# Partition layout of the split keys, a third unit summed by TensorE in batch 1, and a start number for each head

## The chip, the cores and the metric

The kernel runs on one core of one Trainium2 chip. The metric is the device time of one execution in microseconds (us). Before the change three runs gave a median of 877.85 us (877.54 to 879.45).

Five engines work at once, each through its own stream of instructions, and wait for one another by semaphores. PE is TensorE (matrix products, output to the PSUM banks), DVE is VectorE, ACT is ScalarE, POOL is GpSimd, SP is SyncE, which here only starts DMA transfers. ACT starts some too.

## The reference

Four batches, eight heads each, 1152 tokens, head size 64. Neighbouring queries are averaged, so that a head has 576 queries and 1152 keys. What follows the attention is a low-rank mix over tokens and a two-layer MLP.

```python
q_pool = q.reshape(B, H, S // factor, factor, D).mean(axis=3)
scores = scale * np.matmul(q_pool, k.transpose(0, 1, 3, 2))
scores = scores - np.max(scores, axis=-1, keepdims=True)
attn = np.exp(scores)
attn = attn / (np.sum(attn, axis=-1, keepdims=True) + 1e-09)
o = np.matmul(attn, v)                 # heads side by side: x is [4, 576, 512]
h = xt @ U @ V                         # xt is x transposed; U is [576, 32]
u = x + h.transpose(0, 2, 1)
out = u + np.maximum(u @ w_ch1, 0.0) @ w_ch2    # w_ch1 is [512, 2048]
```

## The kernel before

**Split numbers.** PE multiplies in a rounded format. To keep precision an operand is split in a high part (a rounded copy) and a low part (the operand minus the copy), and products of parts are summed in PSUM. For the scores, `T1` holds the high part of the keys in 64 of its 128 partitions and the low part in the other 64; `Q1` holds the high part of the queries twice, in both halves, so that one product (L758) gives high times high plus high times low whichever half holds which. The second product (L759) takes `T2`, the high keys once more and a row of ones, against `Q2`, the low queries and a row with minus the maximum.

**A head** (`head`, n = 8 times batch plus head) goes through these steps. From n = 8 on ("squares"), q and k are loaded as squares of 32 and turned by DVE (L535, L639); ACT copies the turned keys to `T3` (L640), which has one buffer; for each half z ACT writes the high part into `T1` (L643) and DVE or POOL the low part (L644); ACT starts a DMA from `T1` to `T2` (L649). ACT writes `Q1` (L577 to L578, shown as L393), DVE the low queries into `Q2` (L588). PE scans all scores in blocks for their maxima (L695, L697), DVE reduces each block (L701, L706), and a small DMA carries the row of maxima to `Q2`. Then come the scores (L758, L759), ACT's exponential into nine units of 128 keys (L765), the sum of units on DVE or POOL (`add`, L738) and the product with v (L790). Units that `add` leaves out (`LOOSE` of them) are summed by PE, with `ones` as weights, in `total` (L781), once for two heads. L818 and L827 turn the result, L830 to L854 divide it into `X`.

**The tail** of a batch (`tail`) does the low-rank mix (L881 to L903) and then the MLP (L973 on). The MLP of batches 0 to 2 is laid between the heads of the next batch; that of batch 3 stands alone at the end. The weights are decoded from 64-bit input in pieces (`decode`, L429 to L437) during batch 0's MLP.

**The order.** Every step is given to a planner (`Plan`) with a due number `at`, its possible engines with a cost each, and what it reads and writes. The planner replays the program with these costs, takes at each moment the ready step with the lowest due number (`slack` and `bias` bend this), and fixes for each engine the order of its instructions. `dual` offers a step to DVE and POOL. `begin(n)` is the due number at which head n starts and `T` counts from it. So a change of any number can move any instruction. For n < 16 the adds are dealt out by hand: units 1 to 3 go to POOL, the others to DVE.

Of the kernel before, what the change touches and what calls it, by code (L numbers as in the profile page):

```python
# [234 lines left out]
def kernel(  # L235
# [32 lines left out]
    FG = 2  # L268
    QT, KS = -9.2903, -10.0600
    LEAD = 53946.6, 7930.8  # L270
    WHOLE_KEYS, SPLIT = (False, False, True, True), 8
# [3 lines left out]
    TSW, TOT, TSL = 340.0, 325.0, -190.0  # L275
    SUM, AV, YT = 0.6238, 1.1450, 0.7203
# [6 lines left out]
    KT, MX0, MXS = 0.8419, -9.1810, 4.5042  # L283
    V_LO = slice(2 * R, 3 * R)
# [3 lines left out]
    SCALE = 0.5 / float(D) ** 0.5  # L288
    HEAD0, HEAD = 18071.4, 20721.3
    SLOT = HEAD / NG  # L290
    MLP_START, MLP_RATE = 4.9800, (2.0860, 2.0192, 1.7787, 2.0443)
    DEC_START, DEC_LEAD = 84755.4, 14620.3
    SLACK = 16.6000
# [85 lines left out]
    def v_(n):  # L379
        return 1.04 * n + 67  # L380
# [128 lines left out]
    def head(n):  # L509
        op = plan.op if n < len(heads) - 4 else lambda at, ways, r=(), w=(), port=False: plan.op(at, ways, [*r, *arena], w, port)  # L510
        b, h = heads[n]
        par = b % 2
        T = lambda G: begin(n) + G * (SLOT if n >= NWHOLE else SLOT * HEAD0 / HEAD)
        whole = WHOLE_KEYS[b] and not (n >= SQUARES)
# [8 lines left out]
        if squares:  # L523
            qr = lambda: qt.t[:, 0:2 * HALF].rearrange("p (m r d) -> p m r d", r=2, d=32)
            qs = lambda: qt.t[:, 0:HALF]
            for r in range(2):
                for e in range(2):
                    for c in range(2):
                        a = 32 * (2 * e + c)
                        op(T(-17), ("sp", SMALL * dma(36864), lambda a=a, e=e, c=c, r=r: nc.sync.dma_start(  # L530
                            qr()[a:a + 32, :, r], q[b, h, e * NQ:(e + 1) * NQ, 32 * c:32 * c + 32].rearrange("(m p r) d -> r p m d", p=32, r=2)[r]), 0, 1500, BULK), go if n > 1 else [], [(qt, a, r)])
            q_in = [(qt, 32 * a, r) for a in range(4) for r in range(2)]
            op(T(KS - 1), dual(HALF, lambda e: e.tensor_tensor(
                qp.t[:, 0:HALF].rearrange("p (m d) -> p m d", d=32), qr()[:, :, 0], qr()[:, :, 1], op=ALU.add)), q_in, [qp])
            op(T(KS), ("dve", v_(HALF), lambda: nc.vector.transpose(qs(), qp.t[:, 0:HALF])), [qp], q_in)  # L535
# [44 lines left out]
        for e in range(2):  # L580
# [50 lines left out]
        if squares:  # L631
            kr = lambda: kt.t.rearrange("p j (x d) -> p (j x) d", d=32)
            kq = lambda: ks.t.rearrange("p j d -> p (j d)")
            for z in range(2):
                for c in range(2):
                    a = 32 * (2 * z + c)
                    op(T(-17), ("sp", SMALL * dma(73728), lambda a=a, z=z, c=c: nc.sync.dma_start(
                        kr()[a:a + 32], k[b, h, z * S // 2:(z + 1) * S // 2, 32 * c:32 * c + 32].rearrange("(m p) d -> p m d", p=32)), 0, 1800, BULK), go, [(kt, a)])
            op(T(KS + 0.5), ("dve", v_(S // 2), lambda: nc.vector.transpose(kq(), kt.t.rearrange("p j d -> p (j d)"))), [(kt, 32 * a) for a in range(4)], [ks])  # L639
# [184 lines left out]
        def t3():  # L824
# [34 lines left out]
    def tail(b, clock):  # L859
# [339 lines left out]
```

## Time and profile before

| what | value |
|---|---|
| median of 3 runs | 877.85 us |
| the profiled execution, its own time | 877.02 us |
| its span, first to last instruction | 875.2 us |
| PE busy | 864.2 us, 99% |
| DVE busy | 742.4 us, 85% |
| ACT busy | 492.8 us, 56% |
| POOL busy | 252.9 us, 29% |
| granted TensorE clock | 1.000 |

Busy time of PE is not PE at its peak: matrix products are pipelined and their ends are modelled, so that a short wait between two of them can hide in it. The stages are best told apart by stretches of time: heads of batch 0 alone up to about 170 us, then heads of the next batch with the MLP of the one before up to about 700 us, then the MLP of batch 3. A chain of waits follows the work that ended last back from the end, and names for each moment the engine that everything later hung on.

### The profile page before, as it was taken

What the parts mean: (1) busy time and instruction counts of PE and PEld (TensorE: products, weight loads), DVE (VectorE), ACT (ScalarE), POOL (GpSimd) and SP (SyncE); (2) the same over time, 40 slices, a digit from 0 to 9 for tenths busy, and PEclk for the clock granted to TensorE, in tenths of its full rate; (3) what the DMA queues carried; (4) which work ended last, traced back from release to release, by engine and by line L of the source; (5) the groups of instructions that cost most, each with busy time, mean ns of one, the idle gap of its engine ahead of it and who ended that gap; (6) DMA issues with size and microseconds to landing.
All of it is one profiled execution on the core that took longest, in us unless ns stands there. A gap on an engine that the chain in (4) does not pass through costs nothing.

```text
span 875.2 us, 15732 instructions
## 1 busy us (share of the span) xinstructions
PE 864.2 (99%) x5405; PEld 701.7 (80%) x5405; DVE 742.4 (85%) x1508; ACT 492.8 (56%) x1127; POOL 252.9 (29%) x245
## 2 busy tenths in 40 slices
PE   9999998999999999999999999999999999999998
PEld 8787776787777777878888887888887778899987
DVE  8899999999999999978888878788886456798885
ACT  6788978847876876744545555554554322322220
POOL 3445554434443446521211112321402000001110
PEclk9999999999999999999999999999999999999999
DMA  5244645556866776754454453354643325555432
GB/s 172 80 132 110 179 125 136 122 158 185 230 198 190 205 207 186 204 133 121 109 151 104 102 147 95 86 139 122 176 119 102 119 97 185 180 191 191 168 107 99
DMA packets 186646, 128.23 MB, mean 147 GB/s; under 512 B 148139, under 2 KB 161734, under 8 KB 186566
## 3 DMA queue, kind: packets, MB, share of 16 engines
q1 hardware_dynamic: 183942, 117.95, 46.9%
q10 hardware_dynamic: 2624, 9.28, 4.6%
q8 instruction: 43, 0.70, 0.3%
q14 instruction: 37, 0.30, 0.1%
HBM read 96.17 MB, written 21.50 MB: 134 GB/s over the span
## 4 chain that ended last, share of the span: by engine, by line
PE 90%; DVE 5%; ACT 2%; DMA 2%; issue 1%; POOL 0%; SPq 0%; DVEq 0%; ACTq 0%
PE m L1122 22%; PE m L1007 17%; PE m L790 14%; PE s L758 8%; PE s L759 8%; PE m L695 8%; PE s L1051 6%; PE m L781 2%; DVE mp L701 1%; PE m L818 1%; PE m L697 1%; PE m L886 1%; DVE acc L738 1%; PE m L973 1%; PE m L668 1%
## 5 line engine op out<-in xcount | busy, mean ns | idle before, releaser
L765 ACT ACTIVATE big<-s 128x320 f32<-128x320 f32 (+2 forms) x448 | 196.5, 478 | 121.3 <-PE s L759 118.1
L701 DVE TENSOR_REDUCE mp<-m 128x1 f32<-128x384 f32 (+1 forms) x448 | 215.6, 534 | 36.8 <-PE m L695 35.4
L1122 PE MATMUL m<-w,hh 128*128 128x512 f32 x798 | 219.2, 394 | 0.0
L1007 PE MATMUL m<-rest,w 128*128 128x512 f32 (+1 forms) x768 | 178.6, 354 | 0.0
L758 PE MATMUL s<-room 128*128 128x256 f32 (+2 forms) x576 | 166.7, 305 | 0.5
L759 PE MATMUL s<-room 65*128 65x256 f32 (+2 forms) x576 | 163.9, 298 | 1.3 <-DMA room<-mr 1.3
L1122 PEld LDWEIGHTS m<-w,hh 128*128 128x128 f32 x798 | 145.3, 188 | 24.6 <-issue 0.9
L790 PE MATMUL m<-big,v 128*64 128x288 f32 x1152 | 148.5, 410 | 0.1
L1007 PEld LDWEIGHTS m<-rest,w 128*128 128x128 f32 x768 | 131.0, 188 | 13.8 <-issue 1.1
L790 PEld LDWEIGHTS m<-big,v 128*64 128x64 f32 x1152 | 79.1, 137 | 58.5 <-issue 6.8
L695 PE MATMUL m<-room 128*128 128x384 f32 x384 | 122.6, 356 | 2.8 <-DVE acc L738 1.3
L738 DVE TENSOR_TENSOR acc<-acc,big 128x576 f32<-128x576 f32 x133 | 102.7, 772 | 22.9 <-ACT big L765 17.1
L738 POOL TENSOR_TENSOR acc<-acc,big 128x576 f32<-128x576 f32 x67 | 95.6, 1426 | 85.1 <-ACT big L765 57.6
L758 PEld LDWEIGHTS s<-room 128*128 128x128 f32 x576 | 109.2, 190 | 10.8 <-issue 3.5
L759 PEld LDWEIGHTS s<-room 65*128 65x128 f32 x576 | 109.2, 190 | 6.7 <-DMA room<-mr 1.2
L695 PEld LDWEIGHTS m<-room 128*128 128x128 f32 x384 | 69.4, 188 | 23.8 <-issue 5.1
L1126 DVE TENSOR_TENSOR X<-m,X 128x512 f32<-128x512 f32 x95 | 65.0, 684 | 9.9 <-PE m L1122 9.6
L437 POOL TENSOR_TENSOR wt<-wt,rx 128x512 int32<-128x512 int32 (+2 forms) x35 | 45.5, 1302 | 68.8 <-DVE room L588 12.7
L583 POOL CAST qb<-room 64x64 fp32r<-64x64 f32 x54 | 17.7, 328 | 146.7 <-DVE acc L738 71.0
L799 ACT ACTIVATE ay<-m 128x256 f32<-128x256 f32 x48 | 18.4, 383 | 58.2 <-PE m L790 54.1
L1011 ACT ACTIVATE hh<-m 128x512 fp32r<-128x512 f32 (+1 forms) x64 | 32.9, 515 | 27.4 <-PE m L1007 26.4
L738 POOL TENSOR_TENSOR acc<-big 128x576 f32<-128x576 f32 x21 | 30.0, 1427 | 51.1 <-ACT big L765 50.9
(136 smaller groups left out, 1093.2 us busy)
## 6 DMA issues: line engine op xcount, KB each, us to landing
w<-wc SPq DMA_DIRECT2D x96, 512.0 KB, 4.0
rx<-in_moe_w_ch_dram SPq DMA_DIRECT2D x32, 512.0 KB, 4.1
wc<-w SPq DMA_DIRECT2D x32, 512.0 KB, 3.3
v<-in_v_dram SPq DMA_DIRECT2D x32, 288.0 KB, 3.0
room<-room ACTq DMA_DIRECT2D x31, 288.0 KB, 3.2
k<-in_k_dram SPq DMA_DIRECT2D x96, 72.0 KB, 2.2
q<-in_q_dram SPq DMA_DIRECT2D x192, 36.0 KB, 2.4
out_dram<-X SPq DMA_DIRECT2D x11, 256.0 KB, 2.6
```

What stands on the lines that cost most here:

```text
L437: op(at, ("pool", g_(n), lambda: nc.gpsimd.tensor_tensor(tv(), tv(), lo(), op=ALU.add)), [t, (raw, 1)] + use, [t])
L695: nc.tensor.matmul(pm.t[:, 0:w], Q1.t[:, t * P - 64:t * P + 64], T1.t[:, cs_], start=True, stop=True)
L701: op(T(MX0 + 0.3 + MXS * u / 14), ("dve", v_(w), lambda c=c, t=t, w=w, pm=pm: nc.vector.reduce_max(mp.t[:, c * 5 + t:c * 5 + t + 1], pm.t[ ...
L738: ways = dual(NQ, lambda e: e.tensor_tensor(acc.t, a(), b_(), op=ALU.add))
L758: nc.tensor.matmul(o, T1.t[:, kc], Q1.t[:, qa:qz], start=True, stop=False)
L759: nc.tensor.matmul(o, T2.t[:, kc], Q2.t[:, PAD + qa:PAD + qz], start=False, stop=True)
L765: op(T(when + 0.1), ("act", a_(len(js) * nq, True), lambda js=js, qa=qa, qz=qz, nq=nq, ss=ss, p=pu[j], e=js[0] % 2: nc.scalar.activation(p ...
L790: nc.tensor.matmul(pa.t[hf * D:(hf + 1) * D, 0:HALF], vt.t[:, j], pu[j].t[:, j % 2, hf * HALF:(hf + 1) * HALF], start=(j == 0), stop=(j == ...
L1007: op(now, ("pe", mm(nb), lambda c=c, i=i, a=a, bb=bb, w=w, ph=ph, sl=sl: nc.tensor.matmul(ph.t[:, 0:nb], w.t[:, a, c * P:(c + 1) * P], (ul ...
L1051: nc.tensor.matmul(bank.t[:, 0:NB], left(a, c), ub.t[:, i, bb, c], start=(c == 0 and j == 0), stop=(c == 1 and j == 2))
L1122: op(now, ("pe", mm(512), lambda f=f, i=i, a=a, bb=bb, w=w, h_=h_: nc.tensor.matmul(po.t, h_.t[:, a, ns], w.t[:, bb], start=(f == fg and i ...
L1126: op(now, ("dve", v_(512), lambda: nc.vector.tensor_tensor(x(), po.t, x(), op=ALU.add)), [po], bk[t])
```

## The change

In squares the low part of half z of the keys now stays in the partitions that the turned keys have, and the high part is written by ACT into the other half of `T1`. `T2` is filled from `T3`, in two DMAs of half the size that wait for `T3` alone, where one DMA waited for both of L643. The low queries (L588) may go to POOL too when n is 8 or more. `LOOSE` of batch 1 goes from 2 to 3, so that `add` skips one more unit there and `total` sums it. Numbers of the planner become separate for each batch (`PRI`), each head gets a begin of its own (`BEGIN`), and several costs are other numbers.

```diff
-    LOOSE = (1, 2, 0, 0)
+    LOOSE = (1, 3, 0, 0)
...
-    HEAD0, HEAD = 18071.4, 20721.3
+    HEAD0, HEAD = 17993.6, 19715.5
+    BEGIN = (40.0181, 19618.6, 39817.3, 54367.3, 71620.9, 89683.3, 107886.2, 125106.8,
...
-    BIAS, BIAS_FROM = -329.4000, 0.0
+    BIAS, BIAS_FROM = -397.9041, 0.0
...
-        return min(n, NWHOLE) * HEAD0 + max(n - NWHOLE, 0) * HEAD
+        return BEGIN[n]
...
-            op(T(-4.5 if n == 0 else QT + 1.0), ("dve", v_(HALF) + 90, lambda rows=rows, cs_=cs_, e=e: nc.vector.tensor_tensor(
-                Q2.t[0:D, PAD + e * HALF:PAD + (e + 1) * HALF], turned(rows), Q1.t[rows, cs_].bitcast(F32), op=ALU.subtract)),
-               qT_keys + q1[0] + q1[1], [(Q2, e)], port=squares)
+            low = dual(HALF, lambda eng, rows=rows, cs_=cs_, e=e: eng.tensor_tensor(
+                Q2.t[0:D, PAD + e * HALF:PAD + (e + 1) * HALF], turned(rows), Q1.t[rows, cs_].bitcast(F32), op=ALU.subtract), 5 + 119 * e)
+            op(T(-4.5 if n == 0 else QT + 1.0), low if squares else {"dve": low["dve"]}, qT_keys + q1[0] + q1[1], [(Q2, e)], port=squares)
...
-                op(T(QT + 0.6 + KT * z), ("act", a_(S // 2) + z * MOVE, lambda rz=rz, cz=cz: nc.scalar.activation(T1.t[0:D, cz], kq()[rz], AF.Copy)), [ks], [(T1, z, 0)])
+                xz = slice((1 - z) * D, (2 - z) * D)
+                op(T(QT + 0.6 + KT * z), ("act", a_(S // 2) + MOVE, lambda rz=rz, cz=cz, xz=xz: nc.scalar.activation(T1.t[xz, cz], kq()[rz], AF.Copy)), [ks], [(T1, z, 0)])
                 op(T(QT + 0.6 + KT * z), dual(S // 2, lambda e, rz=rz, cz=cz: e.tensor_tensor(
-                    T1.t[D:P, cz], kq()[rz], T3.t[rz].bitcast(F32), op=ALU.subtract)), [ks, (T3, 0)], [(T1, z, 1)])
+                    T1.t[rz, cz], kq()[rz], T3.t[rz].bitcast(F32), op=ALU.subtract)), [ks, (T3, 0)], [(T1, z, 1)])
...
-            op(T(-6), ("act", 500, lambda: nc.scalar.dma_start(T2.t[0:D].bitcast(F32), T1.t[0:D].bitcast(F32)), 4300), [(T1, 0, 0), (T1, 1, 0)],
-               [(T2, p_, z) for p_ in range(2) for z in range(2)])
+            for z in range(2):
+                op(T(-6), ("act", 500, lambda z=z: nc.scalar.dma_start(
+                    T2.t[0:D, z * S // 2:(z + 1) * S // 2].bitcast(F32), T3.t[z * D:(z + 1) * D].bitcast(F32)), 4000), [(T3, 0)],
+                   [(T2, p_, z) for p_ in range(2)])
```

Lines of the kernel after are numbered some 5 to 9 higher: L758 is L767 there, L759 L768, L695 L704, L901 L910, L973 L982, L903 L912, L644 L651, L588 L594, L649 L657.

The first place that shows how the order moves is PE where the tail of batch 0 ends and its MLP begins. L901 is the last product of the low-rank mix (its `X` is written back by L903 on DVE), L973 turns the rows for the MLP, the rows with `room` are scores of a head of batch 1. Before:

```order
L901 MATMUL m3_117<-xs0_107,Vst_69 128x512
L901 MATMUL m1_115<-xs0_107,Vst_69 128x512
L901 MATMUL m4_118<-xs0_107,Vst_69 128x512
L901 MATMUL m2_116<-xs0_107,Vst_69 128x512
L901 MATMUL m3_117<-xs0_107,Vst_69 64x512
L973 MATMUL m0_114<-ident_65,X0_94 128x128 x4
```

And now:

```order
L910 MATMUL m1_115<-xs0_107,Vst_69 128x512
L767 MATMUL s1_112<-room_72 128x320
L768 MATMUL s1_112<-room_72 128x320
L910 MATMUL m2_116<-xs0_107,Vst_69 128x512
...
L910 MATMUL m4_118<-xs0_107,Vst_69 128x512
L767 MATMUL s0_111<-room_72 128x320
L768 MATMUL s0_111<-room_72 128x320
L910 MATMUL m1_115<-xs0_107,Vst_69 128x512
...
L910 MATMUL m2_116<-xs0_107,Vst_69 64x512
...
L982 MATMUL m4_118<-ident_65,X0_94 128x128 x4
```

Scores stand between the five products now; before, the five stood in a row. Counted from the program's start, PE has 4 products of L695, 10 pairs of L758 and L759, 4 of L781 and 4 of L818 more ahead of the first L973 than before.

The second place is DVE around the same moment: L882 and L894 are steps of the low-rank mix, L639 and L535 turn keys and queries, L644 and L588 are low parts. Before:

```order
L738 TENSOR_TENSOR acc0_81<-acc0_81,big_71 128x576
L644 TENSOR_TENSOR room_72<-k1_75,room_72 64x576
L738 TENSOR_TENSOR acc0_81<-acc0_81,big_71 128x576 x2
L533 TENSOR_TENSOR qp0_79<-q0_76 128x288
L535 STREAM_TRANSPOSE q0_76<-qp0_79 128x288
L894 TENSOR_TENSOR xs0_107<-m2_116,xs0_107 32x512
L728 TENSOR_TENSOR mr1_91<-mr1_91 1x64
L639 STREAM_TRANSPOSE k1_75<-k0_74 128x576
L903 TENSOR_TENSOR X0_94<-m3_117,X0_94 128x512
```

And now:

```order
L651 TENSOR_TENSOR room_72<-k1_75,room_72 64x576 x2
L645 STREAM_TRANSPOSE k1_75<-k0_74 128x576
L710 TENSOR_REDUCE mp1_87<-m3_117 128x1
L903 TENSOR_TENSOR xs0_107<-m1_115,xs0_107 32x512
L710 TENSOR_REDUCE mp1_87<-m2_116 128x1
L710 TENSOR_REDUCE mp1_87<-m4_118 128x1
L912 TENSOR_TENSOR X0_94<-m1_115,X0_94 128x512
```

Reductions of the next head's maxima (L710, before L701) now stand ahead of the tail's last steps. Up to the fifth L903 of the program DVE loses 4 of L588, 1 of L644, 2 of L738, 1 of L533 and 1 of L932, and gains 4 of L845, 3 of L701, 1 of L541 and 1 of L555.

Over the whole program the counts are: L781 112 to 128 on PE; L738 144 to 116 on DVE and 88 to 108 on POOL; L588 64 to 51 on DVE and 0 to 13 on POOL; L644 35 to 32 on DVE and 13 to 16 on POOL; L844 21 to 4 on ACT and L845, the same work, 43 to 60 on DVE; DMAs of L649 24 to 48 on ACT; L533 5 to 13 on DVE and 19 to 11 on POOL. No other count of PE's instructions moves. The order counts each of L781 and L790 once, the trace shows two rows for each.

## Rows read from the trace of the kernel before

**Rows 1.** The page, busy us, share of the span, instructions.

```profile
PE 864.2 (99%) x5405; PEld 701.7 (80%) x5405; DVE 742.4 (85%) x1508; ACT 492.8 (56%) x1127; POOL 252.9 (29%) x245
```

**Rows 2.** Stretches of time: busy us and instructions by engine, clock, DMA.

```profile
core 0: us, PE busy (x) PEld busy (x) DVE busy (x) ACT busy (x) POOL busy (x), PEclk, DMA share, GB/s
87.50:112.50 25.00, 24.70 (x182) 19.16 (x181) 24.52 (x53) 23.23 (x58) 14.63 (x15) 1.00 0.63 174
112.50:137.50 25.00, 21.95 (x160) 15.04 (x158) 24.58 (x50) 20.32 (x48) 12.67 (x12) 1.00 0.59 146
137.50:170.50 33.00, 31.58 (x216) 22.66 (x213) 32.02 (x65) 27.67 (x68) 15.05 (x13) 1.00 0.52 121
...
200.00:350.00 150.00, 149.84 (x925) 114.84 (x925) 145.00 (x298) 109.56 (x239) 70.35 (x59) 1.00 0.71 202
350.00:376.00 26.00, 25.39 (x141) 20.39 (x138) 25.36 (x46) 19.50 (x42) 13.65 (x12) 1.00 0.73 222
376.00:640.00 264.00, 264.00 (x1736) 219.91 (x1736) 215.65 (x433) 137.44 (x326) 58.41 (x63) 1.00 0.49 121
```

**Rows 3.** Chain of waits from 137.5 to 170.5 us: shares, then start, us, what.

```profile
by line: DVE mp L701 33.1%; DVE xs L882 9.9%; DVE acc L738 9.1%; DVE wt L435 7.1%; issue 6.9%; DVE room L644 4.6%; DVE k L639 4.3%; DVE room L588 3.3%; DVE qp L533 2.7%; DVE wt L433 2.3%; DVE X L903 2.1%; DVE X L854 2.1%; DVE xs L894 2.1%; 
...
155.10 0.60 DVE wt L435
...
169.23 0.70 DVE X L903
...
169.98 0.45 PE m L901
170.42 0.11 PE m L973
```

**Rows 4.** DVE by line, 75 to 176 us: busy us, mean ns, idle before.

```profile
L701 DVE TENSOR_REDUCE mp<-m 128x1 f32<-128x384 f32 (+1 forms) x87 | 40.8, 533 | 0.6 <-PE m L695 0.4
L738 DVE TENSOR_TENSOR acc<-acc,big 128x576 f32<-128x576 f32 x22 | 17.2, 781 | 0.2
L644 DVE TENSOR_TENSOR room<-k,room 64x576 fp32r<-64x576 f32 x5 | 3.8, 752 | 0.1
L588 DVE TENSOR_TENSOR room<-q,room 64x288 fp32r<-64x288 f32 x6 | 2.7, 448 | 0.1
L845 DVE TENSOR_SCALAR XH<-m,rs 32x64 f32<-32x64 f32 x8 | 2.2, 273 | 0.1
L533 DVE TENSOR_TENSOR qp<-q 128x288 f32<-128x288 f32 x3 | 1.3, 446 | 0.0
L555 DVE TENSOR_TENSOR room<-k,room 128x576 fp32r<-128x576 f32 x1 | 1.1, 1142 | 0.1
L932 DVE TENSOR_TENSOR w<-wt,w 128x512 fp32r<-128x512 f32 x1 | 0.7, 683 | 0.0
```

**Rows 5.** Chain of waits from 95 to 180 us, single products of PE.

```profile
172.66 0.18 PE m L695
172.85 0.15 PE s L758
...
173.63 0.12 PE s L758
```

**Rows 6.** Chain of waits of the whole span, sums of three units for two heads.

```profile
326.96 1.59 PE m L781 x24
```

**Rows 7.** Timeline from 136 us: start, us, engine, line, idle before and its end.

```profile
149.04 1.40 POOL L644 TENSOR_TENSOR room<-k,room 64x576 fp32r<-64x576 f32 x1 [5.15 <-DVE wt L433]
...
149.19 1.80 DVE L435 SCALAR_TENSOR_TENSOR wt<-rx,wt 128x512 int32<-128x512 int32 x1
```

**Rows 8.** Lines 643, 644, 649 and 533: ns min/median/max, first and last start.

```profile
L643 ACT ACTIVATE room<-k x48: 670/683/687, 119.2 to 658.5; 64x576 fp32r<-64x576 f32 x48
...
L644 POOL TENSOR_TENSOR room<-k,room x13: 1400/1418/1433, 135.4 to 658.4; 64x576 fp32r<-64x576 f32 x13
...
L649 ACTq DMA_DIRECT2D room<-room x24: 468/468/499, 121.0 to 659.2; - x24
...
L533 POOL TENSOR_TENSOR qp<-q x19: 798/806/823, 105.6 to 644.3; 128x288 f32<-128x288 f32 x19
```

More of the change, by code (lines that the diff above doesn't have):

```diff
@@ L268 @@
     FG = 2
-    QT, KS = -9.2903, -10.0600
-    LEAD = 53946.6, 7930.8
+    PRI = ((-9.5982, -5.6578, 2.6644, 1.4803, 1.9131, 0.5079, -9.3280, 4.6979, -0.0429, 1.1933, -1.1324),
+           (-9.1287, -12.1929, 1.3999, 1.4630, -1.2304, 1.3157, -9.5372, 4.3359, -0.4696, 2.2321, -0.6516),
+           (-9.3149, -13.6202, 1.9324, 0.7548, 1.5302, 0.6080, -8.2539, 4.4301, -0.7175, 0.8801, -0.6313))
+    LEAD = 65564.7, 4922.5
     WHOLE_KEYS, SPLIT = (False, False, True, True), 8
@@ L275 @@
     TSW, TOT, TSL = 340.0, 325.0, -190.0
-    SUM, AV, YT = 0.6238, 1.1450, 0.7203
     NS = 6
-    LOOSE = (1, 2, 0, 0)
+    LOOSE = (1, 3, 0, 0)
     SCALED = (False, False, False, False)
@@ L282 @@
     APART = (True, True, False, False)
-    KT, MX0, MXS = 0.8419, -9.1810, 4.5042
     V_LO = slice(2 * R, 3 * R)
@@ L288 @@
     SCALE = 0.5 / float(D) ** 0.5
-    HEAD0, HEAD = 18071.4, 20721.3
+    HEAD0, HEAD = 17993.6, 19715.5
+    BEGIN = (40.0181, 19618.6, 39817.3, 54367.3, 71620.9, 89683.3, 107886.2, 125106.8,
[4 rows of a table added]
     SLOT = HEAD / NG
-    MLP_START, MLP_RATE = 4.9800, (2.0860, 2.0192, 1.7787, 2.0443)
-    DEC_START, DEC_LEAD = 84755.4, 14620.3
-    SLACK = 16.6000
-    BIAS, BIAS_FROM = -329.4000, 0.0
+    MLP_START, MLP_RATE = (5.1128, 2.3210, 6.7115, 4.9170), (2.0916, 2.0068, 1.7753, 2.3046)
+    DEC_START, DEC_LEAD = 124728.8, 14126.0
+    SLACK = 10.9665
+    BIAS, BIAS_FROM = -397.9041, 0.0
     def begin(n):
-        return min(n, NWHOLE) * HEAD0 + max(n - NWHOLE, 0) * HEAD
+        return BEGIN[n]
     KEEP = (0, 0, 0)
@@ L396, in copies, with dual @@
         return ways
-    def dual(n, f):
-        return {"dve": (v_(n), lambda: f(nc.vector)), "pool": (g_(n), lambda: f(nc.gpsimd))}
+    def dual(n, f, more=0):
+        return {"dve": (v_(n) + more, lambda: f(nc.vector)), "pool": (g_(n), lambda: f(nc.gpsimd))}
     TP, TPR, MOVE = 109, 84, 130
@@ L512, in head @@
         par = b % 2
+        QT, KS, SUM, AV, YT, KT, MX0, MXS, S1, S2, S3 = PRI[min(b, 2)]
         T = lambda G: begin(n) + G * (SLOT if n >= NWHOLE else SLOT * HEAD0 / HEAD)
@@ L534, in head @@
                 qp.t[:, 0:HALF].rearrange("p (m d) -> p m d", d=32), qr()[:, :, 0], qr()[:, :, 1], op=ALU.add)), q_in, [qp])
-            op(T(KS), ("dve", v_(HALF), lambda: nc.vector.transpose(qs(), qp.t[:, 0:HALF])), [qp], q_in)
+            op(T(KS), ("dve", v_(HALF) + 26, lambda: nc.vector.transpose(qs(), qp.t[:, 0:HALF])), [qp], q_in)
         else:
@@ L638, in head @@
                         kr()[a:a + 32], k[b, h, z * S // 2:(z + 1) * S // 2, 32 * c:32 * c + 32].rearrange("(m p) d -> p m d", p=32)), 0, 1800, BULK), go, [(kt, a)])
-            op(T(KS + 0.5), ("dve", v_(S // 2), lambda: nc.vector.transpose(kq(), kt.t.rearrange("p j d -> p (j d)"))), [(kt, 32 * a) for a in range(4)], [ks])
+            op(T(KS + 0.5), ("dve", v_(S // 2) + 28, lambda: nc.vector.transpose(kq(), kt.t.rearrange("p j d -> p (j d)"))), [(kt, 32 * a) for a in range(4)], [ks])
             op(T(QT), ("act", a_(S // 2), lambda: nc.scalar.activation(T3.t, kq(), AF.Copy)), [ks], [(T3, 0)])
@@ L748, in head @@
                     pu[j + 1] = pu[j]
-                    todo = [((j, j + 1), 0, NARROW, j), ((j,), NARROW, NQ, j + -0.0974), ((j + 1,), NARROW, NQ, j + 1.4230)]
+                    todo = [((j, j + 1), 0, NARROW, j), ((j,), NARROW, NQ, j + S1), ((j + 1,), NARROW, NQ, j + S2)]
                 else:
-                    todo = [((j,), 0, HALF, j), ((j,), HALF, NQ, j + -0.5337)]
+                    todo = [((j,), 0, HALF, j), ((j,), HALF, NQ, j + S3)]
                 for js, qa, qz, when in todo:
@@ L829, in head @@
         op(T(E), ("pe", 3 * TP, t3), [(ay, 2)] + [(ay, "last", e) for e in range(3)], [pz])
-        op(T(E + 0.1), ("dve", 168, lambda: nc.vector.reciprocal(
+        op(T(E + 0.1), ("dve", 214, lambda: nc.vector.reciprocal(
             rs.t[:, :, 0:4], pz.t[:, 0:2 * P].rearrange("p (c e x) -> p e c x", e=2, x=32)[:, :, :, 0])), [pz], [(rs, 2)])
         for e in range(2):
-            op(T(E + 0.1), ("dve", 172, lambda e=e: nc.vector.reciprocal(
+            op(T(E + 0.1), ("dve", 196, lambda e=e: nc.vector.reciprocal(
                 rs.t[32 * e:32 * e + 32, 0, 4:6], pz.t[64:96, 2 * P:3 * P].rearrange("p (f e x) -> p e f x", e=2, x=32)[:, e, :, 0])),
@@ L871, in hkeys @@
             return [k for i in range(H // 2) for e in range(2) for k in ([(X[b], i, e)] if t < 4 else [(XH[b], b, i, f, e) for f in range(2)])]
-        now = begin((b + 1) * H) + MLP_START * SLOT
+        now = begin((b + 1) * H) + MLP_START[b] * SLOT
         ptm = new("m")
@@ L893, in tail @@
         rr = slice(R, 2 * R)
-        op(now, ("dve", v_(DM), lambda: nc.vector.tensor_tensor(
+        op(now, ("dve", v_(DM) + 116, lambda: nc.vector.tensor_tensor(
             ts()[rr], ptm.t[rr], ts()[rr].bitcast(F32), op=ALU.subtract)), [ptm, (z, "s")], [(z, "s")])
```

4 rows, old and new, of the table BEGIN are left out of this document.

## The prediction

> **What bounds the kernel now.** I read the page first: PE is busy 99% of the span [rows 1], so a gain must come out of time in which PE waits or out of work that leaves PE. The second view splits the span into stretches and shows where PE waits [rows 2]. The reader is to subtract PE's busy time from each stretch: 0.30 us missing in 87.5 to 112.5, 3.05 in 112.5 to 137.5, 1.42 in 137.5 to 170.5, 0.16 in 200 to 350, 0.61 in 350 to 376, nothing in 376 to 640. So 4.8 us of PE's time are lost in the last heads of batch 0, and little anywhere after. The clock is granted in full throughout. The third view, the chain of waits in 137.5 to 170.5 [rows 3], says who causes it: reductions (L701), adds, tail steps and low parts on DVE, nearly end to end, until L903 at 169.23 releases L901 on PE at 169.98, behind which the first L973 begins the MLP. DVE is busy 32.02 of the 33 us there [rows 2], and none of its groups has idle time worth a name [rows 4]. From L973 on PE has the MLP's products to fill every gap and is full, though DVE stays busy 145.00 of 150 us. So the kernel has a first stage that ends when DVE has done batch 0's tail, and behind it PE sets the time. What counts in the first stage is how early DVE gets there and how much of PE's work is already done by then.
>
> **Lows in place, highs moved.** The count of copies stays, only the partitions change. Before, L643 wrote in place for one half and across partitions for the other, and all 48 took 670 to 687 ns [rows 8]; so a moved copy costs ACT nothing more, and the layout by itself is worth 0.
>
> **Two DMAs for one.** 24 more issues of 468 ns [rows 8] are 11.2 us on ACT over the run; 17 of L844 leave it for DVE. In 137.5 to 170.5 ACT has 5.3 us free [rows 2] and meets some three heads of batch 1, 1.4 us. The transfers may start before L643 is done, up to two copies (1.4 us) earlier, but PE is not seen waiting for them in the chain of that stage. I take 0; bounds: a gain of 0.5 if a score waits there unseen, a loss of 1.4 if ACT's free time is gone.
>
> **A third unit on PE.** L781 takes 1.59 us for three sums of two heads [rows 6], so 0.53 for one; batch 1 has four such pairs: PE gains 2.1 us of work. Since PE is full there, all of it stays on the path: +2.1. In return eight adds leave DVE.
>
> **The first stage.** The order puts in front of the fifth L903, of which the chain speaks, other work on DVE. It leaves: 4 low queries of 0.448, a low key of 0.752, 2 adds of 0.781, an L533 of 0.446, an L932 of 0.683, together 5.2 us. It gains: 4 L845 of 0.273, 3 reductions of 0.533, an L555 of 1.142 [rows 4], and an L541, which has fewer columns than an add and is estimated at no more than 0.78: together 4.6. DVE gets there 0.6 us earlier. PE meanwhile has done more before the first L973: 4 scans of 0.18, ten pairs of L758 and L759 (0.12 to 0.15 for one of L758 by its shape [rows 5], L759 taken as the same: 2.4 to 3.0, middle 2.7), and four of L781, 0.53; the four small transposes are left out. That is 3.9 us. PE's lost time in this stage falls by 0.6 + 3.9 = 4.5 us. It fits in the 4.8 us that the three stretches lose, and leaves 0.3, which 87.5 to 112.5 loses today with DVE busy 24.52 of 25: so an engine pair as dense as this has a precedent. Bounds: nothing of it, if PE's additional work only fills what DVE's longer queue makes new, and 4.8 plus what hides in modelled ends, some 2 more.
>
> **Behind it.** Up to batch 1's tail, at 350 to 376, DVE is relieved further: 9 low queries, 9 adds, 2 low keys, 3 L932 fewer ahead of its first L903 and a few small steps more, some 11 us by the same rows. PE can get back there only what it loses, 0.16 + 0.61 us visible [rows 2] and about as much unseen: I take -0.9, bounds -2 and +1. In batches 2 and 3 twenty adds and some low parts go to POOL; PE loses nothing there today, and POOL is busy 58.41 of 264 us [rows 2], which covers it: 0 is the value, and the price if that cover fails is the third rival's.
>
> **The sum**, against the profiled execution's own 877.0 us (span 875.2 and 1.8 around it): -4.5 + 2.1 - 0.9 = -3.3, so 873.7. The median of the runs lies 0.8 above that execution: 874.5.
>
> **Rivals.** First, POOL blocks DVE. In the timeline a low key on POOL starts at 149.04 and takes 1.40; L435 on DVE starts at 149.19 and takes 1.80 [rows 7], where another holds the chain for 0.60 [rows 3]. So DVE lost some 1.2 us, on the chain, to 1.40 us of POOL. The change sends four low queries and a low key there that stood on DVE ahead of the tail's end: 4 x 0.806 (the nearest of 288 columns, L533) + 1.418 [rows 8] = 4.6 us of POOL, of which 1.2 in 1.4 would be lost to DVE, 4.0. Then the first stage gains 0.5 where 4.5 was counted, and the time is 877.85 - 0.5 + 2.1 - 0.9 = 878.5. For it: the pair of rows. Against it: the planner links a POOL step behind the last DVE step that uses both, and most low parts of before show their usual time, 0.752 [rows 4]. The Trainium skill, "SBUF — State Buffer", Who interferes with whom, states the rule: a DVE instruction with two inputs in SBUF and a GpSimd instruction that reads SBUF exclude each other, and the second one blocks until the first is done. This pair of rows agrees with it.
>
> Second, it ends slower. In batches 2 and 3 an add on POOL takes about as long as a low key there (576 columns), 1.42, where DVE takes 0.78: 0.64 more for each of twenty, 12.8 us if every one of them is what PE waits for. It decides from the point where a head's last add on POOL ends after PE has come to L781 or a unit's buffer is wanted for the next exponential. If half of them do: 874.5 + 6.4 = 880.9. Against it: 376 to 640 loses nothing today although adds run on POOL there as well, and PE's queue there always holds MLP products.
>
> Third, more comes back: waits that hide in modelled ends go too, 7 us in the first stage instead of 4.5 and 2 behind it: 877.85 - 7 - 2 + 2.1 = 871. For it: DVE's relief of 11 us by batch 1's tail is larger than what I count. Against it: PE is full from 170 on.
>
> That the change does not do what it says is excluded for the third unit and the DMAs, which the order shows; that the new layout saves time by itself is excluded by the equal copies.
>
> **Numbers.** My forecast 0.55 (its own range 872 to 877), POOL blocking DVE 0.18, slower through POOL 0.10, more gain 0.17. The time is the likeliest case's, 874.5. The range from 870 to 879.5 takes in the first and third rival and leaves out the most of the second and the far ends. Faster or slower is meant as over 0.2%, 1.75 us, what a measurement of this kernel can tell: below 876.1 or above 879.6. Faster: 0.43 of the forecast's 0.55, 0.02 of the first rival, all 0.17 of the third: 0.62. Same: 0.12 + 0.12 + 0.01 = 0.25. Slower: 0.04 + 0.09 = 0.13.
>
> **What would show it.** Right: the first L973 starts at about 169.8 us, with the counts above ahead of it; PE's missing time between 112.5 us and that point falls from 4.5 to under 1 us; L781 shows 32 rows for two heads of batch 1 where it showed 24, and such a group takes 2.1 us rather than 1.59; ACT's DMA issues double with the same 468 ns. The first rival is right if L738, L882, L435 or L644 on DVE show means well over those of [rows 4] between 110 and 170 us, beside POOL. The second is right if PE waits for L738 on POOL after 376 us. The forecast is wrong if L973 starts later than today, or if it starts earlier and the time is not lower.

## The result and the profile after

| | before | after |
|---|---|---|
| median of 4 runs each, side by side | 878.63 us (877.54 to 879.45) | 869.98 us (869.64 to 872.03) |
| ratio, 95% interval | 1 | 0.9907 (0.9886 to 0.9928) |
| the profiled execution, its own time | 877.02 us | 869.94 us |
| its span | 875.2 us | 868.1 us |

The change makes the kernel faster by 8 us, where the forecast had 3.3. On another occasion after took 870.85 us, at a ratio of 0.9925 (0.9913 to 0.9937). The direction was right, the size was not: the time is nearest to the third rival's (871), and lies 0.02 us under the lower end of the range.

The page of after answers to [rows 1]:

```profile
PE 860.2 (99%) x5437; PEld 704.2 (81%) x5437; DVE 735.4 (85%) x1494; ACT 490.8 (57%) x1118; POOL 288.4 (33%) x260
```

PE has 32 products more and yet 4.0 us less busy time, in a span that is 7.1 us shorter: busy time itself held waits. The stretches of after, with the columns of [rows 2], the third one up to the first L982:

```profile
87.50:112.50 25.00, 24.61 (x182) 19.07 (x180) 24.50 (x54) 23.04 (x57) 16.59 (x15) 1.00 0.56 146
112.50:137.50 25.00, 23.69 (x165) 17.80 (x161) 23.21 (x48) 20.29 (x51) 16.99 (x15) 1.00 0.55 130
137.50:171.40 33.90, 33.36 (x236) 23.06 (x237) 32.58 (x64) 28.42 (x67) 21.27 (x19) 1.00 0.59 142
200.00:350.00 150.00, 149.59 (x951) 116.21 (x947) 144.21 (x289) 113.72 (x250) 72.57 (x61) 1.00 0.74 210
350.00:376.00 26.00, 26.00 (x166) 20.57 (x165) 23.08 (x43) 15.22 (x35) 14.14 (x13) 1.00 0.66 177
376.00:640.00 264.00, 264.00 (x1726) 223.45 (x1726) 215.22 (x438) 140.09 (x328) 84.47 (x74) 1.00 0.49 123
```

PE's missing time from 112.5 us to the end of the first stage falls from 4.47 to 1.85, and at 350 to 376 from 0.61 to 0. DVE has 2.3 us less to do at 350 to 376, and POOL 26 us more at 376 to 640. Together these stretches miss 5.54 us before and 2.65 after, 2.9 less. What else was gained is in no row of missing busy time.

**Lost time.** To find it I took the starts of PE's products alone. From each product to the next one in order there is a usual gap (at the 40th percentile over all kernels measured here, by the two lines and shapes). What a gap is longer than that is lost. Products of one line that start within 0.03 us of one another (L790 and L781 start so) have to be taken as one start. The floor is arbitrary, so only differences count: a second count with just these rules gives 38.8 and 29.5 for the sums of before and after, and each column falls by the table's amount within 0.2. The sum for each kernel is its usual gaps plus its lost time, and gives its span to the last product. By time (us lost):

| kernel | to 125 | 125–200 | 200–350 | 350–400 | behind 400 | sum |
|---|---|---|---|---|---|---|
| before | 11.9 | 8.2 | 5.2 | 3.9 | 7.7 | 36.9 |
| after | 10.5 | 6.0 | 3.6 | 1.3 | 6.4 | 27.7 |
| after, another run | 11.7 | 5.7 | 3.5 | 1.3 | 6.4 | 28.7 |

Lost time falls by 9.2, work grows by 2.1, together -7.1, the difference of the spans. Two runs of after differ by 1.2 before 125 us and by 0.3 behind it; so the first column decides nothing, and the others do.

**Where the largest unseen piece was.** At 350 to 400 us batch 1 hands over to its MLP. The timeline of before, weight loads of PE, whose idle time before a load is in brackets, with what ended it:

```profile
373.88 0.19 PEld L695 LDWEIGHTS m<-room 128*128 128x128 f32 x1 [0.24 <-ACT rest L982]
374.41 0.19 PEld L695 LDWEIGHTS m<-room 128*128 128x128 f32 x1 [0.35 <-DVE rest L983]
375.01 0.19 PEld L695 LDWEIGHTS m<-room 128*128 128x128 f32 x1 [0.41 <-DVE rest L983]
375.54 0.19 PEld L695 LDWEIGHTS m<-room 128*128 128x128 f32 x1 [0.34 <-issue]
```

Four scans stand one behind the other, and three of them wait until ACT or DVE has emptied the PSUM tile of a turned row. Their starts are 0.5 to 0.6 us apart, where a scan takes 0.18 [rows 5]. The products before them are pipelined and their ends modelled, so that PE passes for busy. The same place in after, its chain of waits from 361 to 372 us, with start, us, what:

```profile
by line: PE m L799 41.1%; PE m L1131 23.8%; PE m L910 11.0%; PE m L982 7.3%; PE s L768 6.0%; PE s L767 5.9%; PE m L790 5.7%
...
362.23 0.94 PE m L910 x4
...
366.13 0.44 PE m L982 x4
366.57 4.52 PE m L799 x36
371.09 0.62 PE m L790 x8
371.71 0.37 PE m L982 x2
```

PE alone carries this chain. Behind the first four L982 stand 36 products with v, 4.52 us in which the tile of the turned row can be emptied.

Behind that place the scans lose less too. Weight loads of the scans in batch 1's MLP, before (375 to 630 us) and then after (371 to 629), with count, busy us, mean ns and idle time:

```profile
L695 PEld LDWEIGHTS m<-room 128*128 128x128 f32 x129 | 23.3, 188 | 7.6 <-ACT ay L800 2.3 <-issue 2.3 <-DVE mp L701 0.5
```

```profile
L704 PEld LDWEIGHTS m<-room 128*128 128x128 f32 x135 | 25.2, 188 | 2.5 <-ACT ay L809 0.5 <-issue 0.5
```

**The first stage.** The end of its chain of waits in after, which answers to [rows 3]:

```profile
166.47 0.60 ACT xs L901
167.07 0.27 ACT ay L808
167.44 0.69 DVE xs L903
168.18 0.50 PE m L910
168.68 0.15 PE s L767
168.83 0.15 PE s L768
168.98 0.29 PE m L910
...
170.81 0.23 PE m L910
```

From 168.18 on PE carries it: scores (L767, L768) lie between the products of L910, where before the fifth L901 stood still for 0.68 us behind an L903. The first L982 starts at 171.36, which is 1.1 later than the first L973 (170.26), with about 4.0 us more of PE's work done by then. That makes 2.9 us less lost. The other run of after starts it at 172.34, so that the 2.9 is known to about 1 us.

### The profile page after: what moved, and what is told of

It is laid out like the page before. It is cut to its first block, busy times and chain, and to the rows that moved or that the text cites. A ratio compares the mean times of both kernels' runs of the same rounds, so it can differ in the third digit from the quotient of the medians.

```text
span 868.1 us, 15815 instructions
## 1 busy us (share of the span) xinstructions
PE 860.2 (99%) x5437; PEld 704.2 (81%) x5437; DVE 735.4 (85%) x1494; ACT 490.8 (57%) x1118; POOL 288.4 (33%) x260
## 4 chain that ended last, share of the span: by engine, by line
PE 89%; DVE 7%; DMA 2%; ACT 1%; issue 1%; SPq 1%; DVEq 0%; ACTq 0%
PE m L1131 22%; PE m L1016 16%; PE m L799 14%; PE s L767 8%; PE s L768 8%; PE m L704 7%; PE s L1060 6%; DVE mp L710 2%; PE m L790 1%; PE m L827 1%; PE m L706 1%; DVE acc L747 1%; DMA k<-in_k_dram 1%; PE m L982 1%; PE m L895 1%
## 5 line engine op out<-in xcount | busy, mean ns | idle before, releaser
L710 DVE TENSOR_REDUCE mp<-m 128x1 f32<-128x384 f32 (+1 forms) x448 | 214.3, 531 | 25.8 <-PE m L704 24.7
L1131 PE MATMUL m<-w,hh 128*128 128x512 f32 x798 | 221.6, 395 | 0.0
L1016 PE MATMUL m<-rest,w 128*128 128x512 f32 (+1 forms) x768 | 182.6, 354 | 0.0
L768 PE MATMUL s<-room 65*128 65x256 f32 (+2 forms) x576 | 163.6, 299 | 1.4 <-DMA room<-mr 1.4
L767 PE MATMUL s<-room 128*128 128x256 f32 (+2 forms) x576 | 163.5, 301 | 0.0
L747 POOL TENSOR_TENSOR acc<-acc,big 128x576 f32<-128x576 f32 x86 | 122.8, 1428 | 114.2 <-ACT big L774 71.6
L704 PE MATMUL m<-room 128*128 128x384 f32 x384 | 122.3, 350 | 1.2 <-ACT room L650 0.3
L767 PEld LDWEIGHTS s<-room 128*128 128x128 f32 x576 | 109.2, 190 | 8.7 <-issue 3.5
L768 PEld LDWEIGHTS s<-room 65*128 65x128 f32 x576 | 109.2, 190 | 6.1 <-DMA room<-mr 1.2
L747 DVE TENSOR_TENSOR acc<-acc,big 128x576 f32<-128x576 f32 x106 | 84.7, 799 | 12.8 <-ACT big L774 11.7
L704 PEld LDWEIGHTS m<-room 128*128 128x128 f32 x384 | 70.0, 188 | 15.4 <-ACT room L398 3.1
L1022 DVE SCALAR_TENSOR_TENSOR hh<-m,hh 128x512 fp32r<-128x512 f32 (+1 forms) x64 | 37.3, 582 | 15.6 <-ACT hh L1020 15.0
L747 POOL TENSOR_TENSOR acc<-big 128x576 f32<-128x576 f32 x22 | 31.4, 1429 | 48.4 <-ACT big L774 29.5
```

Source lines behind the costliest of these rows:

```text
L704: nc.tensor.matmul(pm.t[:, 0:w], Q1.t[:, t * P - 64:t * P + 64], T1.t[:, cs_], start=True, stop=True)
L710: op(T(MX0 + 0.3 + MXS * u / 14), ("dve", v_(w), lambda c=c, t=t, w=w, pm=pm: nc.vector.reduce_max(mp.t[:, c * 5 + t:c * 5 + t + 1], pm.t[ ...
L747: ways = dual(NQ, lambda e: e.tensor_tensor(acc.t, a(), b_(), op=ALU.add))
L767: nc.tensor.matmul(o, T1.t[:, kc], Q1.t[:, qa:qz], start=True, stop=False)
L768: nc.tensor.matmul(o, T2.t[:, kc], Q2.t[:, PAD + qa:PAD + qz], start=False, stop=True)
L1016: op(now, ("pe", mm(nb), lambda c=c, i=i, a=a, bb=bb, w=w, ph=ph, sl=sl: nc.tensor.matmul(ph.t[:, 0:nb], w.t[:, a, c * P:(c + 1) * P], (ul ...
```

## The experiments

Each ratio is to the kernel before on the same chip, with its 95% interval. An edit of after or before is named as such.

**1. The parts with the numbers of before.** After, with PRI, LEAD, MLP_START, MLP_RATE, DEC_START, DEC_LEAD, SLACK and BIAS set back, and:

```diff
-        return BEGIN[n]
+        return min(n, NWHOLE) * HEAD0 + max(n - NWHOLE, 0) * HEAD
```

> The kernel after with all of its parts (low parts in place, two DMAs from T3, low queries on either engine, third unit on TensorE, its step costs), but with the planner's numbers of before (one set for all batches, begins in equal steps, SLACK, BIAS, DEC_START and the rest as before). Before is 878, after 870 us. Theory P (the parts pay: less work on VectorE and GpSimd in its place): 870 to 873. Theory N (the numbers pay: they put TensorE's instructions in another order): 877 to 881, no better than before, since the third unit costs 2 us. Theory T (they pay only together, the numbers being fitted to the parts): 875 to 880.

Measured: 876.14 us, 0.9989 (0.9978 to 1.0000). Lost: 11.2, 9.5, 4.0, 1.5, 6.7. At batch 1's tail and behind it the parts alone bring nearly all that after has; but they lose 1.3 more than before at 125 to 200 us, and pay the 2.1 of the third unit. The 1.3 need not be the order's: TensorE's clock was at 0.66 for 5 us there (the row is in the last section), which is up to 1.7 us.

**2. The numbers with the parts of before.** After, with LOOSE at 2 for batch 1, highs and lows in the old halves, one DMA from `T1`, and low queries on DVE alone.

```diff
-    LOOSE = (1, 3, 0, 0)
+    LOOSE = (1, 2, 0, 0)
...
-            op(T(-4.5 if n == 0 else QT + 1.0), low if squares else {"dve": low["dve"]}, qT_keys + q1[0] + q1[1], [(Q2, e)], port=squares)
+            op(T(-4.5 if n == 0 else QT + 1.0), {"dve": low["dve"]}, qT_keys + q1[0] + q1[1], [(Q2, e)], port=squares)
```

> The kernel after with its numbers for the planner, but with the parts of before: low parts of the keys in the upper half, one DMA from T1, low queries on VectorE alone, two units on TensorE. Theory P: 876 to 880. Theory N: 868 to 872, perhaps a little under after, as 2 us of TensorE's work go. Theory T: 874 to 878. In the trace theory N expects scans that follow a scan (L704 behind L704) without the waits of before in the second and third batch.

Measured: 882.36 us, 1.0059 (1.0047 to 1.0071): slower than before. Lost: 10.3, 14.3, 6.2, 7.1, 6.6. The stretches of this kernel around both tails, columns as in [rows 2]:

```profile
125.00:150.00 25.00, 20.70 (x146) 15.40 (x146) 22.58 (x46) 17.05 (x40) 15.54 (x13) 0.93 0.59 151
350.00:375.00 25.00, 24.16 (x117) 17.57 (x114) 23.67 (x43) 14.07 (x31) 13.43 (x11) 0.90 0.54 161
```

PE starts 117 products at 350 to 375, where after starts 160, and it is called busy for 24.16 us. Part of this is the clock: at 0.93 and 0.90 in these rows, and 0.96 from 375 to 400, it takes up to 25 times 0.21, 5 us, from this execution, the slowest of six (884.8). Four of the six had a mean clock of 0.998, so at most some 1.8 us of such loss, and took 882.20 to 882.38; the numbers alone are thus still 3 us slower than before. So parts alone give -1, numbers alone +3 to +5, and both together -8: no sum of the two, as theory T had it, though no theory had the numbers alone so slow.

**3. The third unit's products left out.** After, in its exact order; `total` does not issue the third unit of batch 1, so that this unit is in no sum.

```diff
-            for i in range(parts):
+            n_sum = parts - (b == 1)
+            for i in range(n_sum):
```

> The kernel after in its exact order on every engine, but of batch 1's sums on TensorE one unit of three is left out (its products are not issued, so batch 1's sums lack that unit). It measures the price of the third unit where it stands: four groups of 0.53 us, 2.1 us less, 867.9, if TensorE is full there and all of it is on the path; 870 if TensorE waits there for something else and the unit is hidden.

Measured: 870.68 us, 0.9919 (0.9907 to 0.9932), not faster than after. Work falls by 2.1, lost time at 200 to 350 rises from 3.6 to 5.3, its old value. The third unit fills time in which PE would wait.

**4. Low queries on DVE at the same place.** After, in its order; the 13 steps that it gives to POOL are issued on DVE.

```diff
+        return {"dve": (v_(n) + more, lambda: f(nc.vector)), "pool": (g_(n), lambda: f(nc.vector))}
```

> The kernel after in its exact order, but the 13 low queries that the planner gave to GpSimd are issued on VectorE at the same place of the order. VectorE gets 13 times 0.45 us more, 5.9 us, six of them near the end of the first stage (heads 9 to 11) when VectorE sets the time. If VectorE's work ahead of batch 0's tail sets the time of the first stage: 1.5 to 3 us slower, 871.5 to 873, and the first L982 later by about that. If GpSimd's hold on the shared port cost as much as it saved: no change, 869.5 to 870.5.

Measured: 878.83 us, 1.0020 (1.0009 to 1.0030). All of the gain is gone, three times what was expected at most; the profiled execution, at full clock, took 877.23. Lost: 10.4, 8.7, 5.2, 3.9, 6.8. At 350 to 375 us, this kernel and then after:

```profile
350.00:375.00 25.00, 22.87 (x123) 18.29 (x123) 24.70 (x41) 13.99 (x31) 12.89 (x11) 1.00 0.58 161
```

```profile
350.00:375.00 25.00, 25.00 (x160) 19.57 (x159) 22.14 (x41) 14.40 (x33) 13.83 (x13) 1.00 0.64 175
```

DVE is full again, and its chain stands before PE's there:

```profile
359.86 0.60 DVE xs L894
360.46 0.67 DVE acc L750
361.13 2.33 DVE mp L713 x5
...
365.05 1.38 DVE xs L894
```

**5. An idle load on DVE, the low queries on POOL.** After, with a maximum over 336 columns of an idle tile (a median of 486 ns) in DVE's queue ahead of each of the 13.

```diff
+            nc.vector.reduce_max(idle[:, 336:337], idle[:, 0:336], axis=AX.X)
+            return f(nc.gpsimd)
```

> The kernel after in its exact order, low queries on GpSimd as in after, but VectorE is given a maximum over 336 columns of an idle tile, which waits for nothing, ahead of each of the 13 places. In the run before, moving the 13 low queries to VectorE cost 9 us. Theory D (VectorE's work sets the time of the first and of the second batch, TensorE's full bars hide waits): 13 times some 0.45 us of work come back as 4 to 7 us, 874 to 877. Theory B (it was the low query's own wait at that place that held up VectorE's queue): 870 to 872.

Measured: 872.06 us, 0.9939 (0.9927 to 0.9950). 13 times 0.486 is 6.3 us of DVE, for 1.2 to 2.1 us of time by the two medians of after. What an idle maximum does not have is a low query's waits for the turned queries and for `Q2`; but these are not what the fourth experiment lost, since its trace shows DVE idle for at most 0.03 us before any of its 48 low queries. Nor was the load the same. The pages, the fourth experiment's and then this one's:

```profile
PE 862.4 (99%) x5437; PEld 704.0 (80%) x5437; DVE 742.4 (85%) x1507; ACT 490.6 (56%) x1118; POOL 280.4 (32%) x247
```

```profile
PE 860.6 (99%) x5437; PEld 704.5 (81%) x5437; DVE 737.3 (85%) x1508; ACT 490.6 (56%) x1118; POOL 289.4 (33%) x260
```

Against after's 735.4 DVE's busy time rises by 7.0 there and by 1.9 here, and the spans of the two executions by 7.3 and 2.1 (875.4 and 870.2 against 868.1). The 13 low queries on DVE took 9.2 us, up to 1.57 for one, where 0.45 is usual; the maxima took 0.459 to 0.503 each, and other steps became shorter. In these two the time goes with DVE's busy time in all. That the added busy time causes it, and not the places where it falls, was not tested by itself.

**6. The old halves.** After, in its order, high keys back in the lower half of `T1` and low keys in the upper.

```diff
-... T1.t[xz, cz] ...
+... T1.t[0:D, cz] ...
...
-... T1.t[rz, cz] ...
+... T1.t[D:P, cz] ...
```

> The kernel after in its exact order, but the high part of the keys goes to the lower half of T1 and the low part to the upper half, as in before; the two DMAs from T3 stay. All theories: the partitions are worth nothing by themselves, 869.5 to 870.8. Should keeping the partitions save VectorE or GpSimd time: 871 to 873.

Measured: 872.78 us (870.98 to 874.17), 0.9941 (0.9928 to 0.9954). After's later runs (869.80 to 871.83) overlap these. Its profile and then after's, from 130 us, columns as before, the clock behind POOL:

```profile
130.00:135.00 5.00, 3.38 (x23) 2.17 (x23) 4.43 (x6) 3.80 (x10) 2.51 (x2) 1.00 0.63 170
135.00:140.00 5.00, 5.00 (x27) 4.96 (x26) 3.50 (x7) 3.23 (x9) 4.85 (x5) 0.66 0.45 99
```

```profile
130.00:135.00 5.00, 4.01 (x28) 3.23 (x25) 3.41 (x7) 4.69 (x12) 4.77 (x4) 1.00 0.44 119
135.00:140.00 5.00, 5.00 (x37) 4.46 (x39) 5.00 (x11) 4.15 (x11) 3.94 (x4) 1.00 0.68 151
```

Where PE had waited 1.6 of 5 us, the clock of the next 5 us was 0.66, between full speed and the lower level (0.5): 5 times 0.34 is 1.7 us. With this loss aside nothing remains for the layout. The six executions say the same: two at a mean clock of 0.999 and 1.000 took 870.98 and 871.15, as after does, and four at 0.998 took 872.32 to 874.17. Whether the old halves bring on that longer wait (after's nine executions all show 1.000) is open.

**7. The third unit alone.** Before, in its exact order; unit 6 of batch 1 is no longer added on DVE but summed by PE.

```diff
+        accs.append([lambda: acc.t] + [unit(j) for j in ((6,) if b == 1 else ())] + [unit(j) for j in loose])
```

> The kernel before in its exact order, but in batch 1 the last add on VectorE is not issued and TensorE sums that unit instead (nothing is left out of the result): 8 adds of 0.78 us leave VectorE, 2.1 us of products come to TensorE. Theory D: 3 to 5 us faster than before, ratio 0.994 to 0.997. The prediction's step (TensorE is full behind the first stage, so the products cost 2.1 us and the adds give nothing): ratio 1.002.

Measured: 876.67 us, 0.9985 (0.9976 to 0.9993). At 200 to 350 it loses 3.4 where before loses 5.2, at batch 1's tail 3.5, hardly less than before. The relief of eight adds pays for the 2.1 us of products, and little more: between theory D and the prediction's step.

**8. The low queries alone.** Before, in its exact order, the same 13 low queries on POOL.

```diff
+... lambda rows=rows, cs_=cs_, e=e, on=nc.gpsimd if (n, e) in LOWS else nc.vector: on.tensor_tensor(
```

> The kernel before in its exact order, but the 13 low queries that after gives to GpSimd (of heads 9, 10, 11, 13, 17, 18, 19, 23, 27, 28) are issued on GpSimd, at their place in the order. VectorE loses 5.9 us of work, some 3 of it ahead of batch 0's tail. Theory D: ratio 0.994 to 0.997. Theory T (it pays only in an order that was planned for it): 0.999 to 1.002, as GpSimd now does them late in an order that does not know it. First rival of the prediction (GpSimd blocks VectorE): 1.000 to 1.003, with adds and steps on VectorE longer beside GpSimd.

Measured: 878.25 us, 1.0014 (1.0005 to 1.0022): a little slower, and at full clock the same (878.13 for four executions, 877.95 for thirteen of before). On POOL they take 0.983 us in the mean (line 589 of this kernel; columns as in [rows 4]):

```profile
L589 POOL TENSOR_TENSOR room<-q,room 64x288 fp32r<-64x288 f32 x13 | 12.8, 983 | 5.4 <-ACT room L394 4.8
```

After's take a median of 0.798. Moving them into an order that was made without them gains nothing.

**9. More for DVE in batches 2 and 3.** After, with two maxima over 288 idle columns in DVE's queue ahead of 28 adds on POOL.

```diff
+                    for _ in range(2):
+                        nc.vector.reduce_max(idle[:, 288:289], idle[:, 0:288], axis=AX.X)
```

> The kernel after in its exact order, but ahead of each of 28 adds of batches 2 and 3 that GpSimd does now and VectorE did before, VectorE gets two maxima over 288 columns of an idle tile, some 0.85 us that wait for nothing: 24 us of work, nearly all in the third batch's stage (366 to 630 us). If VectorE's relief made that stage's gain of 3 us (before lost 7.5 us there by the same count, after 4.3): 3 us or more come back, 873 to 876. If the order made it (the kernel with the numbers alone lost 4.2 there with the adds of before's parts): 870 to 871.

Measured: 890.97 us, 1.0155 (1.0141 to 1.0169). 56 times a median of 0.450 is 25.2 us of DVE for 20.1 us of time, though DVE is busy only 215 of 264 us there without them, and far above either expectation. What PE waits for at 376 to 640 (us in all, times, longest), none of it in after:

```profile
PE m L737 <- DVE mx L719: 3.1, 6, 1.2
PE m L708 <- DVE mp L714: 0.9, 2, 0.5
```

Behind 400 us 22.4 are lost where after loses 6.4. So DVE's free time there is not free at each place: what stands ahead of a head's maxima is late for PE.

**10 and 11. A unit's add left out.** After, in its order: batch 0's last adds (unit 7), then batch 1's (unit 5), not issued on any engine.

```diff
+            ways = dual(NQ, lambda e, out=(b == 0 and j == 7): None if out else e.tensor_tensor(acc.t, a(), b_(), op=ALU.add))
```

> The kernel after in its exact order, but batch 0's last add, of unit 7, is not issued, so batch 0's sums lack that unit: 8 adds of 0.78 us, 6.2 us, leave VectorE in the first stage. If VectorE sets that stage's end: 3 to 5 us less, 865 to 867, with the first L982 earlier by that. If TensorE or a wait for a transfer does: 869 to 870.

> The kernel after in its exact order, but batch 1's last add, of unit 5, is not issued, so batch 1's sums lack that unit: 8 adds, 6.2 us, leave VectorE in the second stage. The run without the third unit's products showed that 2.1 us of TensorE there are hidden. Theory D (VectorE sets the time there): 2 to 4 us less, 866 to 868. If neither engine alone does, both being dense: 0 to 1 us less, 869 to 870.

Measured: 868.82 us, 0.9904 (0.9890 to 0.9917), and 870.29 us, 0.9918 (0.9906 to 0.9931); after beside them had 870.85. The first lies between its two expectations, the second at the smaller gain. Less DVE work in batch 0 is still worth 1 to 2 us, in batch 1 nothing that can be told: with the third experiment, neither the adds nor PE's products alone set that stage's time any more.

**12. After again**, for these comparisons.

> The kernel after once more, beside the others, as the measure for them and for the run with the old halves, which came out at ratio 0.994 where after had 0.991. If that difference is the layout's: 0.991 again here. If it is the clock that TensorE is granted at 135 to 140 us, after a wait of about 1.6 us of five, which after has in some runs as well: some of its runs are near 873 too, and the ratio lies between 0.991 and 0.994.

Measured: 870.85 us, 0.9925 (0.9913 to 0.9937). Its ratio lies between the two, but no execution is near 873 (the highest is 871.83), and each has a mean clock of 1.000. Its lost time is in the table above.

## Why the prediction was right in direction and off in size

**Layout and DMAs, 0: held as far as measured.** The sixth experiment shows no gain of the layout at full clock. The DMA issues of after, in ns (min, median, max):

```profile
L657 ACTq DMA_DIRECT2D room<-room x48: 468/473/1032, 121.2 to 650.4; - x48
```

Two DMAs for one, at the same order, was not tried.

**A third unit, "since PE is full there, all of it stays on the path: +2.1": this step failed.** Its size was right; the chain of after shows one group for two heads with 32 rows in place of the 24 of [rows 6]:

```profile
228.22 2.08 PE m L790 x32
```

But PE was not full. Left out (experiment 3), nothing comes back: kernels with the unit lose 3.4 to 4.4 us at 200 to 350, save the fourth (5.2); before and the kernels of experiments 2 and 3, without it, lose 5.2 to 6.2 (the eighth some 0.3 less than before). 1.7 of its 2.1 us fill waits.

**The first stage, -4.5: PE's work ahead was right, DVE's earlier arrival did not come.** The lost time to the first L982 falls by 2.9. The forecast said that the first L973 would come at 169.8 with 3.9 us more work ahead; it came at 171.36 with 4.0 us more, later than before, which the prediction had named as a sign that it is wrong. PE's missing time from 112.5 us on came to 1.85, where under 1 was the sign for right. So the 3.9 was right, and the 0.6 by which DVE was to be earlier came to nothing: its first L903 stood at 169.23 [rows 3], and in after, with those behind it:

```profile
169.21 2.48 DVE L912 TENSOR_TENSOR X<-m,X 128x512 f32<-128x512 f32 x4
```

The 1.1 by which the first L982 is later is PE's own work between the products of L910. Enough to account for DVE's 0.6 is seen of the first rival, for which the prediction gave the sign to look for; no experiment took it apart. DVE's lines in after, 75 to 176 us, as in [rows 4]:

```profile
L747 DVE TENSOR_TENSOR acc<-acc,big 128x576 f32<-128x576 f32 x20 | 16.9, 845 | 0.1
L891 DVE TENSOR_TENSOR xs<-X,xs 128x512 fp32r<-128x512 f32 x4 | 4.6, 1140 | 0.0
L539 DVE TENSOR_TENSOR qp<-q 128x288 f32<-128x288 f32 x2 | 2.0, 1020 | 0.1
```

L747 takes 845 ns in the mean where L738 took 781, L539 1020 where L533 took 446; L882 had at most 693 for this shape over all of before. One such step in after's timeline:

```profile
143.84 3.65 POOL L651 TENSOR_TENSOR room<-k,room 64x576 fp32r<-64x576 f32 x2
...
146.14 1.90 DVE L891 TENSOR_TENSOR xs<-X,xs 128x512 fp32r<-128x512 f32 x1
```

L891 ends 0.55 us after POOL's second low key, and takes 1.90 where 0.68 is usual. L651 and L440 keep their usual times. 20 times 0.064, 4 times 0.46 and 2 times 0.57 are 4.3 us by which these steps are longer in this stretch. The rival's mechanism is there, at about its price of 4.0, though not all of it fell before the first L982's chain; what it got wrong is that so little else would be gained. The rule of the Trainium skill that the prediction cites ("SBUF — State Buffer", Who interferes with whom) agrees with these rows.

**Behind the first stage, -0.9 and 0: this failed by the most.** Lost time behind 200 us falls by 5.5 us: 1.6 at 200 to 350, 2.6 at 350 to 400, 1.3 later. The 1.6 is the same time as the 1.7 that the third unit fills, and counts once. The prediction bounded it by PE's missing busy time, 0.16 + 0.61. That bound was the mistake: the 0.61 at 350 to 376 stood for 2.8 lost at 350 to 375 alone. At batch 1's tail DVE was the bound, busy 25.36 of 26 [rows 2], as at batch 0's tail, and the prediction had its relief right by count, 11 us; it did not believe it. By time the relief was smaller. DVE up to the first L903 of batch 1's tail, before, and then after up to its L912 (us, busy us and instructions, clock, DMA):

```profile
0.00:368.55 368.55, 348.55 (x731) 1.00 0.60 166
```

```profile
0.00:363.10 363.10, 344.90 (x716) 1.00 0.61 168
```

That is 3.65 us less, not 11. What DVE's steps take beyond their usual times (the medians of before, by line and shape; steps over by more than 0.1 us) sums to 7.1 us up to there before and to 15.8 after, all in steps that overlap one on POOL. The 8.7 more point to the first rival's mechanism, at twice its price, and the gain came in spite of it; no experiment took this apart. With the parts, in either order of numbers, the loss at 350 to 400 is 1.3 to 1.5; with the low queries back on DVE it is 3.9. As the third rival had it, more came back; its "against", that PE is full from 170 on, was the same misreading. That its 871 comes so close is luck: it had 7 in the first stage and 2 behind, where lost time fell by 3.6 up to 200 us and by 5.5 behind.

**Rival two, late adds on POOL, did not happen** (where "Behind it" names the third rival's price for this, the second's is meant). After 376 us PE waits for nothing in after that the profile shows. That this was no matter of course is seen in the ninth experiment, where DVE's time in that stage costs four fifths of itself.

**Not in the prediction: parts and numbers need each other.** The numbers without the relief lose 14.3 us at batch 0's tail and 7.1 at batch 1's, of which the clock can account for 1.8 and 3.5; the relief without the numbers gains at batch 1's tail, and whether it loses at batch 0's is hidden by the clock. Which of the numbers does it stays open, and so does what each gives behind 400 us, where either set of changes brings about 1 us.

## What to carry to other kernels

Where an engine is pipelined and its ends are modelled, as PE here, "busy 100%" is no proof that it doesn't wait: take the distances between the starts of its instructions, or the idle time of its weight loads, before you bound a gain by missing busy time. Where this kernel passes from one kind of work to the next, the engine that empties the first products set the time, though it was at 85% over the whole; the second such place gave back as much as the first. Count a relief by the engine's busy time after the change and not by the steps that leave it: here longer steps, all beside POOL, took back most of 11 us. Plan the move of work to another engine and the order together: here the moved low queries alone gained nothing, and the new numbers alone cost time.

## What the runs showed of the hardware

Ahead of the program's last us TensorE's clock left full speed in five of these profiles, and not in before or after. In experiment 6 the granted clock was 0.66 behind 1.6 us of waiting in 5, as shown there. In experiment 1 PE was busy for 23.20 of the 25 us before this row:

```profile
150.00:155.00 5.00, 4.77 (x19) 3.70 (x18) 4.86 (x10) 3.06 (x8) 2.62 (x4) 0.66 0.72 182
```

In experiments 2, 7 and 8 the mean of 25 us was 0.90 to 0.97 in one to three stretches. Waits of PE thus cost more than their own length in some orders, as in experiment 6, but not in all: beside experiments 5 to 8, ten executions of before at a mean clock of 0.998 took 877.73 in the median, thirteen at 1.000 took 877.95.

Where a step on DVE and one on POOL overlap, either of them can become longer: L891 on DVE took 1.90 as shown, and after's low keys on POOL take a median of 1.425 us and at most 3.467, where before's took at most 1.433 [rows 8].
